# Other banks for layer one's first products, and another order of the steps, in a fused sigmoid attention and two-layer network

## The chip, the cores and the metric

The kernel runs on one core of one Trainium2 chip. The metric is device time in microseconds for one execution; the figure for the kernel before is the median of three runs.

## The reference

Shapes: `q`, `k`, `v` are 8 x 12 x 448 x 64 (batch, heads, sequence, head width), `w_in` is 768 x 2048, `w_out` 2048 x 768, `beta` 2048, all float32. The result is 3584 x 768, float32.

```python
scores = q @ k.transpose(0, 1, 3, 2) / sqrt(64) - log(448)
attn = 1.0 / (1.0 + exp(-scores))              # a sigmoid, no softmax
x = (attn @ v).transpose(0, 2, 1, 3).reshape(8 * 448, 12 * 64)
h = x @ w_in
g = h * (1.0 / (1.0 + exp(-beta * h)))         # swish with a beta for each column
out = g @ w_out
```

## The kernel before

Everything runs in float16 on TensorE (PE) with float32 sums in PSUM. Attention works on groups of four heads, three groups to a batch and 24 in all; group `g` lies in batch `g // 3`. Layer one and layer two run over batches and over tiles of 128 tokens. For the first tokens both layers are plain matrix products; from then on each layer uses a seven-product scheme for 2 x 2 blocks (P1 to P7, lines 377 to 595), which trades products for additions on VectorE (DVE).

The program is written as one list of steps, each of which emits some instructions. Each engine executes its own instructions in the order in which they were emitted, so the list sets the order of every queue at once: PE, DVE, ScalarE (ACT), GpSimd (POOL, which also issues the loads) and SyncE (SP, which issues the stores). A step's name is a letter and numbers:

- `V g.jt`: scores of group `g` for one block of keys into two score tiles, then two sigmoids on ACT (128 x 896 each). `A g`: the product of the weights with `v`, copied from PSUM by DVE.
- `D b.dc`: a plain layer-one product (`dense1`). `O t.half.part`: a plain layer-two product.
- `I b.d.i`: product P`i` of layer one for batch `b` and the pair `d` of column blocks (`wino1`): six matmuls of 224 columns, then an addition on DVE, a copy on ACT (P1) or two sigmoids (P2). `G b.d` and `B b.d.j` are the swish that follows, on ACT and POOL (`weigh_right`, `weigh_below`).
- `U t.i.part`: half of product P`i` of layer two for the tiles `t` and `t+1` (`wino2`): four matmuls of 384 columns, and after the second half an evacuation. P3 stores tile `t`, P4 stores tile `t+1`; so `U10.4.1` issues the stores of tile 11. A tile's store is four DMAs of 96 KB each, and one of 384 KB in the last batch. The last pair's P2 has one pass for each half of its columns (192 at a time).
- `H`, `X`, `S`, `T`: sums of operands for the seven-product scheme, on DVE. `R`: a transpose of `q` or `k` on DVE. `E`: a copy within `v`.
- `Q g`: the two loads of 224 KB for `q` and `k` of group `g`. `K b`: the six loads of `v` for batch `b` (144 and 48 KB). Both go out on POOL's queue.

PSUM has eight banks. During the opening three score tiles of two banks each are held, and two single banks. Then `share_psum(ctx, seconds, 2, N_ONE, 2)` divides them anew: two score tiles, and four single banks under the tags `one0` to `one3`. The function `bank` hands out the tag that has been unused for longest; with `first` = 2 the order begins with `one2`, `one3`, `one0`, `one1`. A tag gets its place in PSUM when its first tile is made, so here the tags got banks 0, 1, 2 and 3 in the order in which they were first asked for: `one2` got bank 0, `one3` bank 1, `one0` bank 2, `one1` bank 3. After the last V, `scores_done` gives the score tiles' four banks to the same pool, as `one4` to `one7`. A bank is held from a product's opening to the `release` in its last evacuation.

Output buffers (`osb`, four of them, pool `outp`) hold both layer one's partial results and layer two's output tiles; one comes free when its stores have landed. Groups of loaded `q` and `k` share three buffers, batches of `v` two.

In the opening, the eight loads of `w_in` (384 KB each) stand on POOL's queue behind the loads of the first batch. The first layer-one products (16 `dense1` of 224 columns, called by `first_half`) start with four, then three, with half visits of scores in between. A dense product's weights are put in one full 128-column load, or, when the next V or A after the step is an A, as two 64-column halves (`tiled`), the way A's own products are tiled.

Of the kernel before, what the change touches and what calls it, by code (L numbers as in the profile page):

```python
# [13 lines left out]
def kernel(  # L14
# [632 lines left out]
    STEPS = """
        R3.1 R3.0 D0.6 D0.12 R4.1 D0.14 D0.7 V3.1 R4.0 D0.13 D0.0 D0.8 V3.0 D0.3 D0.9 V3.3 D0.1
        D0.10 E1 D0.2 Q6 V3.2 D0.4 O0.0.0 D0.5 O0.0.1 O0.0.2 V4.1 O1.0.0 O0.0.3 A3 V4.0 O1.0.1 R5.1
        D0.11 D0.15 O0.0.4 R5.0 V4.2 O0.0.5 S1.1 O0.0.6 O1.0.2 O1.0.3 S1.0 O0.0.7 S2.0 O1.0.4 V4.3  # L650
        O1.0.5 A4 V5.1 O1.0.6 O0.1.0 O0.1.1 O1.1.0 S2.1 Q7 T3.1 O1.0.7 S4.0 T2.1 O0.1.2 V5.0 T3.0
        O0.1.3 O1.1.1 K2 O1.1.2 O1.1.3 O0.1.4 O0.1.5 V5.2 T2.0 O1.1.4 O0.1.6 O0.1.7 R6.1 O1.1.5 R6.0
        A5 O1.1.6 I1.3.1 V6.2 O1.1.7 S4.1 D1.8 R7.0 S3.1 D1.11 T1.1 Q8 V6.0 Q9 D1.3 R7.1 D1.2 X1.0
        V6.1 D1.10 D1.9 E2 K3 D1.1 X1.1 V6.3 T1.0 D1.0 A6 V7.1 I1.3.6 I1.3.2 X1.2 I1.3.5 V7.0 X1.3
        I1.3.7 I1.3.3 I1.2.1 I1.3.4 G1.3 I1.2.6 B1.3.0 V7.2 R8.1 I1.2.5 I1.2.7 R8.0 B1.3.1 I1.2.2
        I1.2.3 I1.2.4 V8.0 U2.1.0 H2.2 B1.2.1 B1.2.0 R9.1 U2.1.1 R9.0 A7 V8.1 H2.0 H2.1 T4.1 T4.0
        U2.7.0 U2.2.0 U2.2.1 Q10 V8.2 U2.5.0 U2.6.0 U2.6.1 X2.0 S3.0 H2.3 E3 V8.3 U2.5.1 A8 G1.2
        X2.1 V9.1 U2.7.1 U2.3.0 U2.3.1 H4.0 I2.0.1 R10.0 V9.2 H4.2 I2.0.6 U2.4.0 I2.0.5 U2.4.1
        I2.0.2 H4.1 I2.0.3 R10.1 X2.2 U4.1.0 V9.0 X2.3 U4.1.1 Q11 G2.0 U4.6.0 U4.6.1 Q12 A9 V10.0
        I2.0.7 H4.3 U4.5.0 U4.7.0 U4.5.1 V10.1 U4.7.1 I2.0.4 B2.0.1 U4.3.0 U4.4.0 U4.2.0 B2.0.0  # L660
        U4.2.1 R11.0 U4.3.1 U4.4.1 R11.1 I2.1.1 V10.2 Q13 Q14 I2.1.6 I2.1.5 I2.1.7 I2.1.2 K4 I2.1.3
        V10.3 I2.1.4 G2.1 B2.1.0 R12.1 I2.2.1 B2.1.1 A10 V11.0 I2.2.6 I2.2.5 R12.0 I2.2.7 I2.2.2
        I2.2.3 I2.3.1 Q15 G2.2 V11.1 I2.3.6 I2.2.4 B2.2.1 B2.2.0 I2.3.5 I2.3.2 R13.1 I2.3.7 I2.3.3
        V11.2 I2.3.4 B2.3.1 U6.1.0 B2.3.0 H6.2 U6.1.1 A11 H6.0 V12.2 U6.2.0 U6.7.0 H6.1 U6.2.1 G2.3
        V12.0 X3.0 U6.5.0 U6.6.0 U6.6.1 X3.1 U6.5.1 H6.3 I3.0.1 U6.7.1 I3.0.6 X3.2 V12.1 H8.0 E4
        R13.0 U6.3.0 U6.3.1 U6.4.0 U6.4.1 I3.0.5 R15.0 Q16 V12.3 H8.2 I3.0.2 A12 H8.1 V13.1 I3.0.3
        R14.0 U8.1.0 U8.1.1 U8.5.0 U8.6.0 G3.0 I3.0.7 U8.6.1 V13.0 X3.3 R15.1 H8.3 U8.2.0 R14.1
        U8.2.1 U8.5.1 U8.7.0 V13.2 U8.7.1 U8.3.0 I3.0.4 U8.4.0 R16.1 B3.0.0 B3.0.1 U8.3.1 V14.0
        U8.4.1 I3.1.1 A13 V14.1 I3.1.6 K5 I3.1.5 I3.1.7 I3.1.2 I3.1.3 I3.2.1 I3.1.4 Q18 I3.2.6 G3.1
        B3.1.0 B3.1.1 I3.2.2 I3.2.5 V14.2 I3.2.7 I3.2.3 Q17 I3.3.1 I3.2.4 G3.2 I3.3.6 I3.3.5 B3.2.0  # L670
        B3.2.1 I3.3.2 I3.3.7 I3.3.3 V14.3 I3.3.4 U10.1.0 B3.3.0 B3.3.1 H10.2 R16.0 U10.1.1 A14 V15.2
# [5 lines left out]
        U12.4.1 Q20 G4.1 V16.3 I4.1.4 A16 B4.1.0 B4.1.1 R19.0 V17.2 I4.2.1 I4.3.1 I4.2.6 I4.2.5
        V17.1 I4.2.2 Q21 I4.2.7 I4.2.3 G4.2 V17.0 I4.2.4 I4.3.6 B4.2.0 I4.3.5 I4.3.7 I4.3.2 B4.2.1
        R20.0 I4.3.3 G4.3 V18.2 I4.3.4 R19.1 A17 I5.0.1 B4.3.0 X5.0 B4.3.1 U14.1.0 V18.0 I5.0.2 X5.1
        I5.0.6 Q22 I5.0.5 U14.1.1 V18.1 X5.2 X5.3 H14.0 I5.0.3 U14.2.0 E6 H14.2 K7 I5.0.7 H14.1  # L680
        V18.3 G5.0 U14.2.1 A18 V19.2 I5.0.4 U14.6.0 U14.5.0 U14.7.0 B5.0.0 U14.6.1 U14.5.1 B5.0.1
        U14.7.1 I5.1.1 V19.0 H14.3 I5.1.6 I5.1.2 U14.3.0 R21.1 U14.3.1 R20.1 V19.1 U14.4.0 E7 I5.1.5
        I5.1.7 U14.4.1 I5.1.3 V20.0 R21.0 I5.1.4 G5.1 B5.1.0 I5.2.1 B5.1.1 A19 V20.2 I5.2.6 Q23
        I5.2.5 I5.2.2 I5.2.7 I5.2.3 I5.3.1 I5.2.4 G5.2 I5.3.6 B5.2.0 V20.3 I5.3.5 I5.3.7 B5.2.1
        I5.3.2 I5.3.3 I5.3.4 V20.1 X6.0 B5.3.1 H16.2 B5.3.0 U16.1.0 U16.1.1 A20 V21.2 U16.2.0 H16.0
        U16.7.0 U16.2.1 G5.3 V21.0 H16.1 U16.5.0 R23.1 U16.6.0 U16.6.1 H16.3 U16.5.1 U16.7.1 H18.2
        I6.0.1 X6.2 V21.1 U16.3.0 X6.1 U16.3.1 U16.4.0 U16.4.1 I6.0.6 R22.1 I6.0.2 R22.0 I6.0.5 A21
        V22.0 H18.0 X6.3 I6.0.3 H18.1 U18.1.0 U18.7.0 U18.1.1 V22.1 I6.0.7 U18.6.0 U18.6.1 V22.2
# [6 lines left out]
        X7.3 H22.2 H22.1 U20.4.1 U22.5.0 I7.0.6 I7.0.5 U22.7.0 I7.0.7 I7.0.3 U22.6.0 G7.0 I7.0.4
        I7.1.1 I7.1.6 I7.1.5 B7.0.0 B7.0.1 I7.1.2 I7.1.7 I7.2.1 I7.1.3 I7.2.6 G7.1 I7.1.4 I7.2.5
        I7.2.7 B7.1.0 B7.1.1 U22.6.1 I7.2.2 I7.2.3 U22.5.1 H22.3 I7.2.4 I7.3.1 I7.3.6 B7.2.0 I7.3.5
        G7.2 B7.2.1 I7.3.7 U22.7.1 I7.3.2 I7.3.3 U24.1.0 I7.3.4 U22.3.0 U22.3.1 U24.1.1 U22.4.0
        B7.3.0 U22.4.1 U24.2.0 B7.3.1 H24.0 U26.1.0 U24.2.1 H24.1 U24.5.0 G7.3 U24.6.0 H24.2 U24.6.1
# [138 lines left out]
```

## Time and profile before

| | |
|---|---|
| median of three runs | 369.06 us (368.25 to 369.5) |
| profiled execution | 368.85 us |
| its span | 367.1 us |
| PE busy | 360.9 us (98%), 3677 matmuls |
| DVE, ACT, POOL busy | 74%, 68%, 42% |
| granted PE clock | 0.999 |
| store of 96 KB, median issue to landing | 2.4 us (all stores: 1.8 to 6.8) |

The span runs from the first to the last instruction of the profiled execution; 1.75 us of its time lie outside. Start times in the profile's rows count from the start of the span. In a row of the timeline the bracket gives the idle time ahead of it and what ended that. In a row of windows there come the window, its length, and then busy time and instructions of PE, weight loads, DVE, ACT and POOL, the granted clock, the DMA share and GB/s. A row of the chain of waits gives start, duration, and the engine with its line. `L168` is the matmul of every dense product, so rows are told apart by their operands and times.

### The profile page before, as it was taken

What the parts mean: (1) busy time and instruction counts of PE and PEld (TensorE: products, weight loads), DVE (VectorE), ACT (ScalarE), POOL (GpSimd) and SP (SyncE); (2) the same over time, 40 slices, a digit from 0 to 9 for tenths busy, and PEclk for the clock granted to TensorE, in tenths of its full rate; (3) what the DMA queues carried; (4) which work ended last, traced back from release to release, by engine and by line L of the source; (5) the groups of instructions that cost most, each with busy time, mean ns of one, the idle gap of its engine ahead of it and who ended that gap; (6) DMA issues with size and microseconds to landing.
All of it is one profiled execution on the core that took longest, in us unless ns stands there. A gap on an engine that the chain in (4) does not pass through costs nothing.

```text
span 367.1 us, 9125 instructions
## 1 busy us (share of the span) xinstructions
PE 360.9 (98%) x3677; PEld 237.7 (65%) x3677; DVE 272.1 (74%) x521; ACT 249.0 (68%) x409; POOL 154.3 (42%) x192
## 2 busy tenths in 40 slices
...
GB/s 165 175 196 201 195 206 200 234 52 2 50 139 52 158 154 2 68 69 103 163 13 150 52 138 51 50 80 88 52 1 88 2 88 2 0 88 0 60 66 135
...
## 3 DMA queue, kind: packets, MB, share of 16 engines
...
q8 instruction: 29, 0.48, 0.5%
q14 instruction: 13, 0.11, 0.1%
...
## 4 chain that ended last, share of the span: by engine, by line
PE 89%; DMA 6%; POOL 1%; DVE 1%; ACT 1%; issue 0%; SPq 0%; ACTq 0%; DVEq 0%; POOLq 0%
PE m_ps L168 70%; PE sco L215 10%; PE av_ps L288 9%; DMA w_in<-in_moe_w_in_dram 3%; DMA raw<-in_k_dram 2%; DMA out_dram<-osb 1%; POOL w_in L150 1%; POOL raw L112 1%; DVE osb L369 0%; ACT attnT L227 0%; SPq L599 0%; ACT osb L422 0%; DVE xT L297 0%; DVE osb L564 0%; ACT osb L460 0%
## 5 line engine op out<-in xcount | busy, mean ns | idle before, releaser
L227 ACT ACTIVATE attnT<-sco 128x896 f16<-128x896 f32 (+1 forms) x163 | 139.2, 907 | 38.0 <-PE sco L215 37.3
L369 DVE TENSOR_TENSOR osb<-m_ps,osb 128x448 f32<-128x448 f32 (+2 forms) x197 | 116.4, 597 | 50.3 <-PE m_ps L168 41.5
L168 PEld LDWEIGHTS <-w_in 128*128 128x128 f16 (+1 forms) x948 | 80.7, 100 | 19.4 <-issue 11.0
L168 PE MATMUL m_ps<-xT,w_in 128*128 128x224 f16 (+3 forms) x750 | 85.7, 266 | 0.6 <-DVE xT L297 0.5
L489 POOL TENSOR_TENSOR gt<-osb,sg 128x448 f16<-128x448 f32 x26 | 29.6, 1137 | 117.7 <-ACT sg L422 107.8
L499 POOL TENSOR_TENSOR gt<-osb,sg 128x448 f16<-128x448 f32 x52 | 58.3, 1138 | 35.3 <-ACT sg L422 33.7
L422 ACT ACTIVATE sg<-osb,beta_sb 128x224 f32<-128x224 f32 (+1 forms) x104 | 54.0, 575 | 10.3 <-DVE osb L369 10.0
L168 PEld LDWEIGHTS <-sum 128*128 128x128 f16 (+1 forms) x444 | 39.9, 99 | 27.4 <-issue 3.6
L168 PEld LDWEIGHTS <-gt 128*128 128x128 f16 (+1 forms) x474 | 37.0, 102 | 25.8 <-issue 7.5
L168 PE MATMUL m_ps<-w_out,gt 128*128 128x384 f16 (+2 forms) x350 | 52.6, 324 | 0.1
L215 PE MATMUL sco<-qT,kT 32*128 32x448 f16 (+3 forms) x864 | 51.4, 340 | 0.7 <-DVE kT L201 0.6
L168 PEld LDWEIGHTS <-w_S 128*128 128x128 f16 (+1 forms) x486 | 43.9, 99 | 7.0 <-issue 6.0
L168 PE MATMUL m_ps<-w_out,sum 128*128 128x384 f16 (+1 forms) x228 | 40.6, 327 | 0.0
L168 PE MATMUL m_ps<-w_T,sum 128*128 128x384 f16 (+1 forms) x216 | 40.3, 327 | 0.0
L297 DVE CAST xT<-av_ps 128x448 f16<-128x448 f32 (+1 forms) x54 | 28.4, 567 | 14.1 <-PE av_ps L288 13.9
L288 PE MATMUL av_ps<-attnT,v 128*64 128x448 f16 (+3 forms) x400 | 38.2, 343 | 0.0
L168 PE MATMUL m_ps<-xs,w_S 128*128 128x224 f16 (+1 forms) x330 | 36.2, 260 | 0.0
L288 PEld LDWEIGHTS <-v 128*64 128x64 f16 (+1 forms) x432 | 20.4, 108 | 17.7 <-issue 9.8
L422 ACT ACTIVATE osb<-m_ps,beta_sb 128x224 f32<-128x224 f32 x52 | 20.5, 449 | 15.1 <-PE m_ps L168 14.0
L215 PEld LDWEIGHTS <-kT 32*128 32x128 f16 (+1 forms) x864 | 13.5, 96 | 23.2 <-issue 21.1
L460 ACT COPY osb<-m_ps 128x448 f32<-128x448 f32 x26 | 13.8, 536 | 17.7 <-PE m_ps L168 15.3
L317 DVE TENSOR_TENSOR gt<-m_ps,sg 128x224 f16<-128x224 f32 (+1 forms) x40 | 16.6, 434 | 12.1 <-ACT sg L314 11.9
...
## 6 DMA issues: line engine op xcount, KB each, us to landing
...
w_in<-in_moe_w_in_dram POOLq DMA_DIRECT2D x8, 384.0 KB, 11.1
w_out<-in_moe_w_out_dram POOLq DMA_DIRECT2D x4, 768.0 KB, 12.6
...
```

The source lines that it names most:

```text
L112: nc.gpsimd.dma_start(out=raws[g][:, r, c0:c1].rearrange("p c d -> p (c d)"), in_=(q, k)[r][b, HQ * t : HQ * (t + 1)].rearrange("h (p c) d ...
L168: nc.tensor.matmul(to[c : c + step], hidden[:, c : c + step], weights, **({} if step == P else {"tile_position": (0, c)}), **flags,)
L215: nc.tensor.matmul(sco[base : base + nk, hh, u0 : u0 + n], kT[g][lo : lo + BLK, jt * P : jt * P + nk, e], qT[g][lo : lo + BLK, c0 : c0 + n ...
L227: nc.scalar.activation(out=at[:, :, 0:n], in_=sco[:, :, 0:n], func=AF.Sigmoid, bias=NEG_LOG_S, scale=MSCALE,)
L288: nc.tensor.matmul(av[hh * D : (hh + 1) * D, 0:n], vs[b][base : base + nk, 2 * (s % NPAIR) + hh, jt], at[base : base + nk, hh, 0:n], start ...
L297: nc.vector.tensor_copy(out=xTs[b][:, s % NPAIR, c0 : c0 + n], in_=av[:, 0:n])
L317: nc.vector.tensor_tensor(out=gt[:, dc, off : off + n], in0=m1[:, 0:n], in1=sg[:, 0:n], op=ALU.mult)
L369: nc.vector.tensor_tensor(out=out, in0=in0, in1=in1, op=op)
L422: nc.scalar.activation(out=out, in_=in_, func=AF.Sigmoid, bias=0.0, scale=beta_sb[:, dc : dc + 1])
L460: nc.scalar.copy(out=oa[:, 0], in_=m)
L489: nc.gpsimd.tensor_tensor(out=gt[:, 2 * d : 2 * d + 2, off : off + QH], in0=ob[:, 0], in1=sg, op=ALU.mult)
L499: nc.gpsimd.tensor_tensor(out=gt[:, dc, off : off + S].rearrange("p (h n) -> p h n", h=2), in0=oa[:, :, j], in1=sg, op=ALU.mult,)
```

## The change

`share_psum` gets a loop that, where `first` is not zero (only the second call), makes one tile of each of the tags `one0` to `one3` in order, before any is used. So the tags lie in banks 0, 1, 2, 3 by their numbers, and the first products, which still ask for `one2` and `one3` first, lie in banks 2 and 3. In the opening the third score tile held these two; banks 0 and 1 were the two single ones.

The table `STEPS` holds the same 762 steps in another order. The parts that are spoken of below are shown; the rest is permuted in the same manner.

```diff
@@ share_psum
         used.clear()
         used.update(((i + first) % n_one, i - n_one) for i in range(n_one))
+        if first:
+            for i in range(n_one):
+                psum["one"].tile([P, S], FP32, tag=f"one{i}", name="place")
@@ STEPS
...
-        O1.0.5 A4 V5.1 O1.0.6 O0.1.0 O0.1.1 O1.1.0 S2.1 Q7 T3.1 O1.0.7 S4.0 T2.1 O0.1.2 V5.0 T3.0
...
-        V6.1 D1.10 D1.9 E2 K3 D1.1 X1.1 V6.3 T1.0 D1.0 A6 V7.1 I1.3.6 I1.3.2 X1.2 I1.3.5 V7.0 X1.3
...
-        I1.2.3 I1.2.4 V8.0 U2.1.0 H2.2 B1.2.1 B1.2.0 R9.1 U2.1.1 R9.0 A7 V8.1 H2.0 H2.1 T4.1 T4.0
...
-        R13.0 U6.3.0 U6.3.1 U6.4.0 U6.4.1 I3.0.5 R15.0 Q16 V12.3 H8.2 I3.0.2 A12 H8.1 V13.1 I3.0.3
-        R14.0 U8.1.0 U8.1.1 U8.5.0 U8.6.0 G3.0 I3.0.7 U8.6.1 V13.0 X3.3 R15.1 H8.3 U8.2.0 R14.1
-        U8.2.1 U8.5.1 U8.7.0 V13.2 U8.7.1 U8.3.0 I3.0.4 U8.4.0 R16.1 B3.0.0 B3.0.1 U8.3.1 V14.0
-        U8.4.1 I3.1.1 A13 V14.1 I3.1.6 K5 I3.1.5 I3.1.7 I3.1.2 I3.1.3 I3.2.1 I3.1.4 Q18 I3.2.6 G3.1
...
-        U10.2.0 H10.0 U10.7.0 H10.1 G3.3 U10.2.1 U10.5.0 U10.6.0 U10.6.1 H10.3 U10.5.1 X4.0 V15.0
-        U10.7.1 X4.1 U10.3.0 U10.3.1 I4.0.1 I4.0.6 I4.0.5 H12.0 U10.4.0 X4.2 U10.4.1 X4.3 I4.0.2
-        I4.0.3 I4.0.7 V15.1 E5 K6 G4.0 Q19 H12.2 U12.1.0 H12.1 U12.1.1 A15 R17.0 V16.1 U12.2.0 R18.1
...
-        I6.1.4 B6.1.0 I6.2.6 I6.2.5 B6.1.1 I6.2.2 V23.1 I6.2.7 I6.2.3 I6.3.1 I6.2.4 I6.3.6 G6.2
-        B6.2.1 I6.3.5 B6.2.0 I6.3.7 I6.3.2 I6.3.3 V23.2 I6.3.4 B6.3.1 U20.1.0 H20.2 U20.1.1 A23
-        U20.7.0 B6.3.0 U22.1.0 H20.0 U20.2.0 H20.1 X7.0 U20.2.1 U20.5.0 U20.6.0 G6.3 U20.6.1 I7.0.1
...
-        U24.5.1 H24.3 H26.0 U24.7.0 U24.7.1 U26.1.1 U24.3.0 U24.3.1 H26.1 U24.4.0 U26.2.1 U26.5.0
-        U26.6.0 H26.2 U26.6.1 U26.5.1 H26.3 U26.7.0 U26.7.1 U24.4.1 U26.3.0 U26.3.1 U26.4.0 U26.4.1
-        U26.2.0
...
+        V4.3 O1.0.5 A4 K2 V5.2 S2.1 O0.1.0 O1.1.0 O1.1.1 S4.1 O0.1.1 O0.1.2 O1.0.6 V5.0 O0.1.3
+        O0.1.4 O1.1.2 X1.0 T3.0 O1.0.7 O0.1.5 V5.1 O1.1.3 O1.1.4 T3.1 O0.1.6 T2.1 O0.1.7 A5 I1.2.1
...
+        I1.3.1 A6 V7.0 I1.2.7 I1.3.2 I1.3.6 R8.1 V7.1 I1.3.5 I1.2.4 I1.3.7 B1.2.0 I1.3.3 B1.2.1 V7.2
+        I1.3.4 U2.1.0 R8.0 U2.1.1 R9.1 R9.0 B1.3.0 B1.3.1 V8.0 A7 U2.2.0 V8.2 H2.2 U2.2.1 U2.7.0
...
+        E4 U6.4.0 H6.3 I3.0.2 R13.0 I3.0.5 U6.3.0 U6.3.1 I3.0.3 U6.4.1 V12.3 H8.0 H8.1 I3.0.7 A12
+        V13.1 I3.0.4 G3.0 Q16 U8.1.0 H8.2 U8.1.1 U8.6.0 U8.6.1 U8.5.0 R15.1 R14.1 U8.5.1 U8.7.0
+        V13.0 U8.2.0 H8.3 U8.2.1 U8.7.1 V13.2 U8.3.0 R14.0 B3.0.1 U8.3.1 U8.4.0 U8.4.1 B3.0.0 I3.1.1
+        R15.0 Q17 A13 V14.1 I3.1.6 I3.1.5 I3.1.2 I3.1.7 I3.1.3 K5 I3.2.1 I3.1.4 G3.1 B3.1.1 I3.2.6
...
+        A14 H10.1 V15.0 X4.0 R16.0 U10.2.0 Q19 R16.1 U10.2.1 G3.3 U10.5.0 Q18 I4.0.1 U10.6.0 U10.6.1
+        V15.1 X4.1 U10.5.1 I4.0.6 U10.7.1 I4.0.2 H10.3 E5 I4.0.5 H12.2 V15.2 U10.3.0 X4.2 I4.0.3
+        H12.0 X4.3 U10.4.0 U10.3.1 H12.1 U10.4.1 V16.0 I4.0.7 A15 V16.1 I4.0.4 K6 B4.0.1 U12.1.0
+        R17.1 U12.6.0 R18.1 U12.1.1 U12.6.1 U12.7.0 V16.2 U12.2.0 H12.3 R17.0 G4.0 B4.0.0 U12.5.0
...
+        G6.1 I6.1.4 I6.2.6 B6.1.0 I6.2.5 I6.2.7 B6.1.1 I6.2.2 V23.1 I6.3.1 I6.2.3 I6.2.4 B6.2.0 G6.2
+        I6.3.6 B6.2.1 I6.3.5 I6.3.7 I6.3.2 V23.0 I6.3.3 U20.1.0 I6.3.4 H20.2 U22.1.0 U20.1.1 B6.3.1
+        B6.3.0 A23 U20.7.0 U20.2.0 U20.2.1 H20.0 H20.1 X7.0 G6.3 I7.0.1 U20.5.0 U20.6.0 U20.6.1
...
+        U26.6.0 U26.6.1 U26.5.0 H26.3 U26.5.1 U24.4.0 U26.7.0 U26.3.0 U26.7.1 U26.3.1 U24.4.1
+        U26.4.0 U26.4.1 U26.2.0
```

More of the change, by code (lines that the diff above doesn't have):

```diff
@@ L647 @@
     STEPS = """
-        R3.1 R3.0 D0.6 D0.12 R4.1 D0.14 D0.7 V3.1 R4.0 D0.13 D0.0 D0.8 V3.0 D0.3 D0.9 V3.3 D0.1
-        D0.10 E1 D0.2 Q6 V3.2 D0.4 O0.0.0 D0.5 O0.0.1 O0.0.2 V4.1 O1.0.0 O0.0.3 A3 V4.0 O1.0.1 R5.1
-        D0.11 D0.15 O0.0.4 R5.0 V4.2 O0.0.5 S1.1 O0.0.6 O1.0.2 O1.0.3 S1.0 O0.0.7 S2.0 O1.0.4 V4.3
-        O1.0.5 A4 V5.1 O1.0.6 O0.1.0 O0.1.1 O1.1.0 S2.1 Q7 T3.1 O1.0.7 S4.0 T2.1 O0.1.2 V5.0 T3.0
-        O0.1.3 O1.1.1 K2 O1.1.2 O1.1.3 O0.1.4 O0.1.5 V5.2 T2.0 O1.1.4 O0.1.6 O0.1.7 R6.1 O1.1.5 R6.0
@@ L653 @@
-        A5 O1.1.6 I1.3.1 V6.2 O1.1.7 S4.1 D1.8 R7.0 S3.1 D1.11 T1.1 Q8 V6.0 Q9 D1.3 R7.1 D1.2 X1.0
-        V6.1 D1.10 D1.9 E2 K3 D1.1 X1.1 V6.3 T1.0 D1.0 A6 V7.1 I1.3.6 I1.3.2 X1.2 I1.3.5 V7.0 X1.3
-        I1.3.7 I1.3.3 I1.2.1 I1.3.4 G1.3 I1.2.6 B1.3.0 V7.2 R8.1 I1.2.5 I1.2.7 R8.0 B1.3.1 I1.2.2
-        I1.2.3 I1.2.4 V8.0 U2.1.0 H2.2 B1.2.1 B1.2.0 R9.1 U2.1.1 R9.0 A7 V8.1 H2.0 H2.1 T4.1 T4.0
-        U2.7.0 U2.2.0 U2.2.1 Q10 V8.2 U2.5.0 U2.6.0 U2.6.1 X2.0 S3.0 H2.3 E3 V8.3 U2.5.1 A8 G1.2
-        X2.1 V9.1 U2.7.1 U2.3.0 U2.3.1 H4.0 I2.0.1 R10.0 V9.2 H4.2 I2.0.6 U2.4.0 I2.0.5 U2.4.1
@@ L659 @@
[L659 to L664, printed above, removed]
@@ L665 @@
-        V12.0 X3.0 U6.5.0 U6.6.0 U6.6.1 X3.1 U6.5.1 H6.3 I3.0.1 U6.7.1 I3.0.6 X3.2 V12.1 H8.0 E4
-        R13.0 U6.3.0 U6.3.1 U6.4.0 U6.4.1 I3.0.5 R15.0 Q16 V12.3 H8.2 I3.0.2 A12 H8.1 V13.1 I3.0.3
-        R14.0 U8.1.0 U8.1.1 U8.5.0 U8.6.0 G3.0 I3.0.7 U8.6.1 V13.0 X3.3 R15.1 H8.3 U8.2.0 R14.1
-        U8.2.1 U8.5.1 U8.7.0 V13.2 U8.7.1 U8.3.0 I3.0.4 U8.4.0 R16.1 B3.0.0 B3.0.1 U8.3.1 V14.0
-        U8.4.1 I3.1.1 A13 V14.1 I3.1.6 K5 I3.1.5 I3.1.7 I3.1.2 I3.1.3 I3.2.1 I3.1.4 Q18 I3.2.6 G3.1
-        B3.1.0 B3.1.1 I3.2.2 I3.2.5 V14.2 I3.2.7 I3.2.3 Q17 I3.3.1 I3.2.4 G3.2 I3.3.6 I3.3.5 B3.2.0
@@ L671 @@
-        B3.2.1 I3.3.2 I3.3.7 I3.3.3 V14.3 I3.3.4 U10.1.0 B3.3.0 B3.3.1 H10.2 R16.0 U10.1.1 A14 V15.2
-        U10.2.0 H10.0 U10.7.0 H10.1 G3.3 U10.2.1 U10.5.0 U10.6.0 U10.6.1 H10.3 U10.5.1 X4.0 V15.0
-        U10.7.1 X4.1 U10.3.0 U10.3.1 I4.0.1 I4.0.6 I4.0.5 H12.0 U10.4.0 X4.2 U10.4.1 X4.3 I4.0.2
-        I4.0.3 I4.0.7 V15.1 E5 K6 G4.0 Q19 H12.2 U12.1.0 H12.1 U12.1.1 A15 R17.0 V16.1 U12.2.0 R18.1
-        I4.0.4 B4.0.0 U12.6.0 B4.0.1 U12.2.1 U12.5.0 V16.2 U12.6.1 U12.5.1 I4.1.1 H12.3 I4.1.6
-        U12.7.0 U12.7.1 R17.1 I4.1.5 U12.3.0 U12.3.1 I4.1.2 V16.0 R18.0 I4.1.3 U12.4.0 I4.1.7
@@ L677 @@
[L677 to L688, printed above, removed]
@@ L689 @@
-        I6.0.4 H18.3 U18.5.0 G6.0 U18.2.0 R23.0 U18.5.1 U18.2.1 B6.0.1 B6.0.0 U18.7.1 V22.3 U18.3.0
-        U18.3.1 U18.4.0 U18.4.1 I6.1.1 I6.1.6 A22 V23.0 I6.1.5 I6.1.7 I6.1.2 I6.1.3 I6.2.1 G6.1
-        I6.1.4 B6.1.0 I6.2.6 I6.2.5 B6.1.1 I6.2.2 V23.1 I6.2.7 I6.2.3 I6.3.1 I6.2.4 I6.3.6 G6.2
-        B6.2.1 I6.3.5 B6.2.0 I6.3.7 I6.3.2 I6.3.3 V23.2 I6.3.4 B6.3.1 U20.1.0 H20.2 U20.1.1 A23
-        U20.7.0 B6.3.0 U22.1.0 H20.0 U20.2.0 H20.1 X7.0 U20.2.1 U20.5.0 U20.6.0 G6.3 U20.6.1 I7.0.1
-        U20.5.1 H20.3 X7.2 U22.1.1 U20.7.1 I7.0.2 X7.1 U20.3.0 U20.3.1 U22.2.0 U22.2.1 H22.0 U20.4.0
@@ L695 @@
[L695 to L699, printed above, removed]
-        U24.5.1 H24.3 H26.0 U24.7.0 U24.7.1 U26.1.1 U24.3.0 U24.3.1 H26.1 U24.4.0 U26.2.1 U26.5.0
@@ L701 @@
-        U26.6.0 H26.2 U26.6.1 U26.5.1 H26.3 U26.7.0 U26.7.1 U24.4.1 U26.3.0 U26.3.1 U26.4.0 U26.4.1
-        U26.2.0
+        R3.1 R3.0 D0.7 D0.11 D0.0 R4.0 D0.3 V3.0 D0.4 D0.6 D0.14 R4.1 D0.9 V3.2 D0.2 D0.1 V3.3 D0.8
+        Q6 E1 D0.5 D0.12 V3.1 S1.0 D0.10 S2.0 O1.0.0 O1.0.1 O0.0.0 O1.0.2 V4.1 S1.1 Q7 O0.0.1 A3
+        R5.1 V4.2 O0.0.2 O1.0.3 D0.13 D0.15 V4.0 O0.0.3 R5.0 O0.0.4 O0.0.5 O0.0.6 S3.1 O1.0.4 O0.0.7
+        V4.3 O1.0.5 A4 K2 V5.2 S2.1 O0.1.0 O1.1.0 O1.1.1 S4.1 O0.1.1 O0.1.2 O1.0.6 V5.0 O0.1.3
@@ new lines @@
+        O0.1.4 O1.1.2 X1.0 T3.0 O1.0.7 O0.1.5 V5.1 O1.1.3 O1.1.4 T3.1 O0.1.6 T2.1 O0.1.7 A5 I1.2.1
+        R6.1 R6.0 X1.1 T1.0 O1.1.5 O1.1.6 O1.1.7 D1.3 D1.9 T2.0 Q8 I1.2.2 V6.0 I1.2.6 D1.8 I1.2.5 Q9
+        V6.1 T1.1 D1.11 D1.1 V6.2 R7.1 E2 R7.0 I1.2.3 D1.2 Q10 K3 D1.10 V6.3 X1.3 D1.0 G1.2 X1.2
+        I1.3.1 A6 V7.0 I1.2.7 I1.3.2 I1.3.6 R8.1 V7.1 I1.3.5 I1.2.4 I1.3.7 B1.2.0 I1.3.3 B1.2.1 V7.2
+        I1.3.4 U2.1.0 R8.0 U2.1.1 R9.1 R9.0 B1.3.0 B1.3.1 V8.0 A7 U2.2.0 V8.2 H2.2 U2.2.1 U2.7.0
@@ new lines @@
+        H2.0 H2.1 U2.5.0 V8.1 U2.6.0 T4.0 Q12 S4.0 X2.0 U2.6.1 U2.5.1 V8.3 H2.3 T4.1 U2.7.1 G1.3
+        R10.1 A8 V9.2 U2.3.0 U2.3.1 X2.1 X2.2 I2.0.1 S3.0 U2.4.0 V9.0 R10.0 I2.0.6 X2.3 I2.0.5
+        U2.4.1 E3 I2.0.2 I2.0.7 I2.0.3 H4.0 V9.1 U4.1.0 H4.2 I2.0.4 H4.1 A9 V10.2 U4.7.0 U4.1.1
+        U4.6.0 U4.6.1 U4.5.0 U4.5.1 U4.7.1 Q11 B2.0.1 G2.0 H4.3 V10.0 U4.2.0 U4.2.1 B2.0.0 U4.4.0
+        U4.3.0 U4.3.1 R11.0 I2.1.1 R11.1 V10.1 U4.4.1 I2.1.6 I2.1.5 K4 R12.0 I2.1.2 I2.1.7 I2.1.3
+        V10.3 I2.1.4 R12.1 B2.1.1 G2.1 Q13 I2.2.1 A10 V11.0 I2.2.6 B2.1.0 I2.2.5 I2.2.7 I2.2.2
```

27 lines of the change are left out of this document (added).

## The prediction

> **What bounds the kernel now.** I read the page's busy shares first, then the chain of waits, then what PE itself waited for, then the timeline where the table changes.
>
> ```profile
> PE 360.9 (98%) x3677; PEld 237.7 (65%) x3677; DVE 272.1 (74%) x521; ACT 249.0 (68%) x409; POOL 154.3 (42%) x192
> PE 89%; DMA 6%; POOL 1%; DVE 1%; ACT 1%; issue 0%; SPq 0%; ACTq 0%; DVEq 0%; POOLq 0%
> 24.60:363.60 339.00, 338.81 (x3414) 225.87 (x3406) 261.70 (x490) 230.73 (x383) 138.23 (x164) 1.00 0.52 88
> ```
>
> The third line is a window from just behind the opening to the last product: PE is busy 338.81 of 339.00 us at a granted clock of 1.00. An order of issue can take nothing from such a stretch except PE's stalls, and can only add new ones. So I look for stalls, and for what the opening waits for.
>
> ```profile
> 13.23 10.52 DMA w_in<-in_moe_w_in_dram
> 23.80 0.75 PE m_ps L168 x6
> ...
> 154.74 4.52 PE m_ps L168 x32
> 159.28 0.57 DVE osb L564
> 159.89 2.76 PE m_ps L168 x16
> ...
> 171.50 5.43 DMA out_dram<-osb
> 177.11 0.78 ACT osb L422 x2
> ...
> 181.37 0.73 PE m_ps L168 x6
> ```
>
> The chain leaves PE in three places that matter. At 23.80 the seventh product of layer one starts when a chunk of `w_in` lands. At 159.89 and 181.37 PE waits for an evacuation (DVE's copy of U8.1.1, then I3.3.3's adds) that had itself waited for an output buffer whose stores were still under way: Q16's loads stood beside the stores of U6.4.1 (5.8 to 6.5 us to landing, against 1.8 to 1.9 for those of U10.4.1, which had no load beside them), K5 and Q18 beside those of U8.4.1. Measured as excess over the usual spacing of matmul starts they are 0.21 us each; other spots (V3.3 0.06, some 0.04 four times) bring the sum of stalls behind the opening to 0.64 us.
>
> **Part one, the banks.** The loop adds no instruction; it fixes which memory the tags name. Before, tags got memory in order of first use.
>
> ```profile
> 18.99 0.39 DVE L297 CAST xT<-av_ps 128x224 f16<-128x224 f32 x1 [0.23 <-PE av_ps L288]
> 19.30 0.84 DVE L781 STREAM_TRANSPOSE beta_sb<-beta_in 32x32 f32<-32x32 f32 x4
> 19.43 1.41 PE L168 MATMUL m_ps<-xT,w_in 128*128 128x224 f16 x13 [0.48 <-DVE xT L297]
> 20.23 0.45 ACT L314 ACTIVATE sg<-m_ps,beta_sb 128x224 f32<-128x224 f32 x1 [1.13 <-PE m_ps L168]
> ```
>
> So the first product lay where the last `av_ps` was, and started 0.05 after the cast of 18.99 to 19.38 had read it (as an input that cast is read only by the sixth matmul of the product, 5 x 0.096 = 0.48 us in). After, it lies in a bank of the third score tile, whose sigmoids are done at 16.84 + 2.26 = 19.10, so it can start near 19.15: 0.28 earlier. I value that at nothing, because two waits stand behind it. The first sigmoid (20.23) needs `beta_sb`, done at 20.14, whatever PE does; and the seventh product can't start before 23.80, where the chunk lands (the load engines were busy since the start and POOL's order is unchanged there). PE waited 0.31 there; it will wait 0.59. Without that cover the gain would be the 0.28. The chunks behind it land at 26.3, 28.3, 30.3 and 32.3, close behind PE, so nothing is made up later.
>
> **Part two, the table.** The same 762 steps, permuted; DVE, ACT, POOL and SP run the same instructions as before. PE: steps between a V and the next A run as 64-column pairs, and the new order has 22 more matmuls for that. A pair costs what one full matmul does (96 ns for 224 columns, 163 for 384), but each entry from a dense product to scores costs about 0.1 us more and each exit as much. Summing the start-to-start intervals of every adjacent pair, taken class by class from the old trace, gives the new order +0.1 us.
>
> *Old stalls removed:* Q16 now stands behind G3.0 on POOL's queue, laid out some 4 us after U6.4.1's stores have gone, and the steps around the others differ: up to -0.64.
>
> *New stalls.* I laid the new order end to end, each instruction by its kind's mean duration and spacing in this trace. The two largest are late. In batch 6 the old table has I6.2.3, I6.3.1, I6.2.4, I6.3.6; the new has I6.2.3, I6.2.4, I6.3.6, with I6.3.1 ahead of all.
>
> ```profile
> 303.59 0.74 PE L168 MATMUL m_ps<-xT,w_S 128*128 128x224 f16 x6
> 303.79 1.27 DVE L369 TENSOR_TENSOR osb<-m_ps,osb 128x448 f32<-128x448 f32 x2 [0.93 <-PE m_ps L168]
> 304.17 0.74 PE L168 MATMUL m_ps<-xT,w_in 128*128 128x224 f16 x6
> 304.74 0.74 PE L168 MATMUL m_ps<-xs,w_in 128*128 128x224 f16 x6
> 305.32 0.93 PE L168 MATMUL m_ps<-xs,w_S 128*128 128x224 f16 x8
> ```
>
> These are those four products at 0.576 us each (6 x 96 ns). I6.3.6 opens the bank that I6.2.3 leaves, and it is free when DVE's add (0.62) has read it: last matmul's start 0.48, to DVE 0.30, 0.62, back 0.05: 1.45 us after I6.2.3 starts. Three products gave 1.73; two give 1.15. Stall: 0.30.
>
> The other is U22.1.0, now five steps after V23.0. With the visits over, it takes the first bank that the score tiles held, and V23.0's second tile is still to be read there: ACT has V23.0's two sigmoids (0.92 each) behind B6.2.0's, which wait for I6.2.4's add. By the layout ACT is through 6.7 us after I6.2.3's start, PE is there at 6.2 (the 0.30 included): 0.56 with the hand-over. Before, U20.1.1, A23 and U20.7.0 stood ahead of it. Smaller: V5.1, with only two steps to V5.0 where each visit needs two score tiles read (0.13), V7.1 and V8.0 0.03 each. Sum 1.05.
>
> *The end.* U24.4.1 stores a whole tile.
>
> ```profile
> L599 SPq DMA_DIRECT2D out_dram<-osb x105: 314/421/1568, 63.9 to 364.1; - x105
> DMA to landing us min/median/max: 1.8/2.5/6.8
> ```
>
> The 1568 ns is that issue; it began at 360.3 with U26.3 and U26.4 still to run. Now only U26.4.0, U26.4.1 and U26.2.0 come behind U24.4.1, some 2.0 us (4 + 4 matmuls at 0.163, 8 at 0.082), and SP comes to the last stores late: +0.22. The last landing beside 384 KB could cost up to 1.0 (the page has 3.6 us to landing for 384 KB, 2.6 for 192 KB); I take 0, since the large one leaves first.
>
> *Loads beside stores.* Elsewhere the new places of Q and K are between 0 and the rival below; I take +0.15, near the lower end, since most stores get free stretches.
>
> Weighed against one rule: the Trainium skill, Perfetto Trace Analysis, Identifying the Most-Contended Engine, says that matmul busy time is a poor measure and that weight-load busy time is the better one. By its 65% a new order could gain much; the rows above (a product every 0.576 us, no gap) show TensorE streaming, so I give it no term.
>
> **Sum:** +0.1 - 0.64 + 1.05 + 0.22 + 0.15 = +0.9 us. The profiled execution took 368.85 (span 367.1 and 1.75 around it), 0.21 under the median of 369.06; so 369.75 by the profile, 370.0 for the median. Measurement can tell about 0.3%, 1.1 us.
>
> **Rivals.**
>
> *B, slower: stores of U10.4.1 caught by K6.* U12.1.1's copy reuses the buffer that U10.4.1 stores. Four stores of 96 KB go out near 201 us; laid out, PE waits one for one once they take more than 3.0 us to land. Alone they took 1.9. Before, K6 went out at 190.2 with nothing ahead; now Q18's 448 KB are issued just ahead of it on POOL's queue (which runs ahead of PE here, so K6 leaves before U10.4.1 although the list has it behind) and K6 leaves some 2 us later: its last issue is near 195, and with 4.8 us to landing as before, or the 6.0 that the page has for such pieces, it is down at 200 to 201. At the 3.3 to 3.9 us of U10.3.1's stores before, which had K6 beside them, +0.3 to +0.9; at U6.4.1's 5.8 to 6.5, +2.8 to +3.5. I take the near row's end, +0.9: 370.9. It decides once K6's last piece lands after 201. Against it: the old stores with K6 just gone took 1.9.
>
> A rule beside it: the Trainium skill, DMA: Bandwidth & Descriptors, Queues, rings and completion order, has each DMA engine take turns between the queues that it has work for; equal turns would double 1.9 us to an estimated 3.8, +0.8. U10.3.1's rows agree; U6.4.1's tripled time doesn't, so the larger end stays in the range.
>
> *C: the two late stalls don't come.* If the score tiles lie the other way round in the late banks, or ACT has a little more room than I gave it, U22.1.0 is free at once; with an add's usual overlap I6.3.6 also loses its 0.30. -0.86: 369.1.
>
> *D: the change does what its first part says on the path.* If the first product's 0.28 passes through (the `w_in` chunks landing earlier) and both late stalls are also absent: 368.8. The DMA row of 10.52 us speaks against it.
>
> **Chances.** Forecast 0.45, B 0.28, C 0.15, D 0.06, a visit that waits longer for its score tiles than laid out 0.06. An error of some 0.5 us in the sum of stalls puts 0.10 of the forecast over +1.1; of B 0.26 lies there, and the last case whole: slower 0.42. Faster needs D or C with that error on top: 0.08. Same 0.50. The range reaches down to D less 0.6 for the error of the sum, 368.2, and up to 372.0, between B's two prices; its far end I leave out, since it needs K6 beside the stores on their whole way.
>
> **What would show it.** In the new profile: PE busy 98% again; the first `m_ps` near 19.15 and the seventh product still near 23.8; no wait of U8.2.0 on L564; a PE gap of about 0.3 at I6.3.6 and 0.5 at U22.1.0, the second with ACT's sigmoid L227 as releaser; the last 1.57-us issue of SP beginning about 362.4. If the opening's first sigmoid or the seventh product moves forward, part one is wrong; if `out_dram<-osb` shows as releaser of U12.1.1's copy, B holds; if PE has a gap over 0.6 that I haven't named, the layout failed there.

## The result

| | before | after |
|---|---|---|
| median of 20 runs | 368.73 us (368.19 to 369.5) | 369.76 us (369.09 to 371.39) |
| ratio to before | | 1.0029, 95% interval 1.0019 to 1.0039 |
| profiled execution, span | 368.85, 367.1 us | 370.58, 368.8 us |

The kernel after is slower by 1.03 us (0.29% by the ratio); the forecast sum was +0.88, written as 370.0 against 369.06. So the size came out, but part of it for the wrong reasons, as the experiments show. Profile against profile it did not: 370.58 us, where the forecast had 369.75 for the profiled execution.

The page of the kernel after, busy shares and chain, and the same kind of window as before, from behind the opening to the last product:

```profile
PE 362.4 (98%) x3699; PEld 237.9 (65%) x3699; DVE 272.2 (74%) x521; ACT 248.4 (67%) x409; POOL 154.0 (42%) x192
PE 87%; DMA 6%; ACT 2%; POOL 2%; DVE 1%; issue 1%; SPq 0%; ACTq 0%; DVEq 0%; POOLq 0%
24.60:365.20 340.60, 339.21 (x3431) 225.79 (x3428) 261.18 (x490) 230.12 (x383) 137.88 (x164) 1.00 0.53 88
```

PE was idle for 0.19 us of this stretch before and is for 1.39 now; ACT and POOL hold 2% of the chain each, where they held 1%. The stretch itself is longer by more, since PE that waits for a bank can show as busy with the matmul ahead of it; so a gap below is what a step's matmul starts come late, by the usual spacing for each pair of shapes in the trace of before, added up over the step. (Some expectations below name 0.39 us for V5.1 and 0.75 for V20.3; these added up single matmuls of a step of which later ones catch up. By the step they are 0.21 and 0.61. U22.1.0's 0.62 is that of its first matmul; the step comes to 0.65.)

The chain of waits between 170 and 182 us:

```profile
170.50 0.45 SPq L602
...
171.00 6.19 DMA out_dram<-osb
...
177.38 0.52 ACT osb L425 x2
...
181.64 0.73 PE m_ps L171 x6
```

This stands in the place of the row of 171.50 before: U8.4.1's last store takes 6.19 us (5.43 before), I3.2.2's sigmoids wait for its buffer, and PE loses 0.23 us at I3.3.2 and 0.81 at I3.3.3, where it lost 0.21 before. The forecast had it gone.

The timeline at the end of batch 6, PE and then ACT:

```profile
305.04 0.74 PE L171 MATMUL m_ps<-xT,w_S 128*128 128x224 f16 x6
305.61 0.74 PE L171 MATMUL m_ps<-xs,w_in 128*128 128x224 f16 x6
306.56 1.31 PE L171 MATMUL m_ps<-xs,w_S 128*128 128x224 f16 x12 [0.21 <-DVE osb L372]
...
311.91 1.49 PE L171 MATMUL m_ps<-w_out,gt 128*64 128x384 f16 x16 [0.46 <-ACT attnT L230]
```

```profile
310.14 1.71 ACT L230 ACTIVATE attnT<-sco 128x896 f16<-128x896 f32 x2
```

Here are the two stalls that were laid out: I6.3.6 starts 306.56 - 305.61 = 0.95 us after I6.2.4 instead of 0.576 (stall 0.37, forecast 0.30), and U22.1.0 at 311.91, 0.06 after ACT has read V23.0's second score tile at 311.85 (stall 0.65, forecast 0.56).

The opening, PE's timeline of the kernel after:

```profile
18.40 0.69 PE L291 MATMUL av_ps<-attnT,v 128*64 128x224 f16 x8
19.31 2.46 PE L171 MATMUL m_ps<-xT,w_in 128*128 128x224 f16 x24 [0.21 <-ACT attnT L230]
```

The first product waits 0.21 us for the score tile's sigmoid, where it waited 0.48 for a cast. In this execution the seventh product again waited for its chunk, by 0.26. (By the measure of the step, which takes in the delay of the first matmul beside the engine's idle time, the first product's two waits are 0.28 and 0.55 us.)

### The profile page after: what moved, and what is told of

Read it like the earlier page. It is cut to its first block, busy times and chain, and to the rows that moved or that the text cites. A ratio compares the mean times of both kernels' runs of the same rounds, so it can differ in the third digit from the quotient of the medians.

```text
span 368.8 us, 9179 instructions
## 1 busy us (share of the span) xinstructions
PE 362.4 (98%) x3699; PEld 237.9 (65%) x3699; DVE 272.2 (74%) x521; ACT 248.4 (67%) x409; POOL 154.0 (42%) x192
## 4 chain that ended last, share of the span: by engine, by line
PE 87%; DMA 6%; ACT 2%; POOL 2%; DVE 1%; issue 1%; SPq 0%; ACTq 0%; DVEq 0%; POOLq 0%
PE m_ps L171 67%; PE sco L218 10%; PE av_ps L291 9%; DMA w_in<-in_moe_w_in_dram 3%; DMA raw<-in_k_dram 2%; DMA out_dram<-osb 2%; ACT sg L425 1%; ACT attnT L230 1%; DVE osb L372 1%; POOL w_in L153 1%; POOL raw L115 1%; POOL gt L502 1%; ACT osb L425 0%; SPq L602 0%; ACT osb L463 0%
## 5 line engine op out<-in xcount | busy, mean ns | idle before, releaser
L171 PE MATMUL m_ps<-xT,w_in 128*128 128x224 f16 (+3 forms) x768 | 84.8, 266 | 0.4 <-ACT attnT L230 0.2
L136 POOL DMA_DIRECT2D v<-in_v_dram x32 | 19.9, 636 | 13.4 <-DMA w_out<-in_moe_w_out_dram 6.8
```

What stands on the lines that cost most here:

```text
L136: nc.gpsimd.dma_start(out=vs[b][i * BLK : (i + 1) * BLK, :, 0:JF].rearrange("p h j d -> p h (j d)"), in_=rows[:, :, JF * i * D : JF * (i + ...
L171: nc.tensor.matmul(to[c : c + step], hidden[:, c : c + step], weights, **({} if step == P else {"tile_position": (0, c)}), **flags,)
```

## Experiments

Theory: PE is the bound, so the change is worth the sum of its stalls; the late ones come from hand-offs of banks, the one near 180 us from loads beside stores, and the opening's gain ends at the `w_in` chunk. Rivals: the banks themselves cost or win, stalls that are removed turn up elsewhere, or SP and not the loads makes the stores late. Every kernel was timed against the kernel before on its own chip, so ratios are what compares; kernels behind the first four were chosen after those.

| kernel | median us | ratio to before | interval | gaps in its profile, us |
|---|---|---|---|---|
| loop, old table | 368.45 | 0.9991 | 0.9981 to 1.0002 | U8.2.0 0.11 |
| same, again | 368.47 | 0.9986 | 0.9973 to 0.9998 | U8.2.0 0.35, I3.2.2 and I3.3 0.73 |
| new table, no loop | 369.78 | 1.0027 | 1.0015 to 1.0039 | V5.1 0.21, I3.3 0.73, I6.3.6 0.37, U22.1.0 0.65 |
| after, again | 369.59 | 1.0018 | 1.0006 to 1.0031 | V5.1 0.21, I3.3 0.36, I6.3.6 0.37, U22.1.0 0.65 |
| end of batch 6 repaired | 369.06 | 1.0005 | 0.9990 to 1.0019 | V5.1 0.21, I3.3 0.97 |
| K5 later | 370.08 | 1.0036 | 1.0023 to 1.0049 | V5.1, I6.3.6, U22.1.0 as after; U10.5 and U10.7 0.61 |
| K5 early | 369.37 | 1.0016 | 1.0007 to 1.0025 | V5.1, I6.3.6, U22.1.0 as after; I5.3 and V20.3 0.61 |
| K5 and K7 early | 369.45 | 1.0007 | 0.9997 to 1.0017 | V5.1, I6.3.6, U22.1.0 as after |
| repairs, K5 early | 368.34 | 0.9990 | 0.9982 to 0.9999 | I5.3 and V20.3 0.74 |
| old table freed | 368.33 | 0.9984 | 0.9974 to 0.9993 | O0.0.0 0.54 |
| repairs, K5 and K7 early | 368.05 | 0.9983 | 0.9973 to 0.9993 | none over 0.08 |

### The loop alone, twice

```diff
 (the table of before)
+        if first:
+            for i in range(n_one):
+                psum["one"].tile([P, S], FP32, tag=f"one{i}", name="place")
```

> The kernel before with the loop in share_psum alone, its table unchanged. Theory (the opening waits for a w_in chunk anyway): the first layer-one product starts about 0.28 us sooner after the last av_ps product than before, the seventh product still starts when its chunk lands (23.6 to 23.8), and the time is that of before within 0.15 us. Rival (the gain is carried through): 0.28 us less, and a seventh product 0.28 us earlier. Other rival (the banks change a hand-off later on): a new PE gap behind the opening, a time over 0.3 us longer.

Both medians lie under before, by 0.39 and 0.49 us; the first run's interval still reaches 1.0002. The profile of that run shows a reason; PE's timeline:

```profile
19.29 2.46 PE L171 MATMUL m_ps<-xT,w_in 128*128 128x224 f16 x24 [0.21 <-ACT attnT L230]
21.68 0.58 PE L218 MATMUL sco<-qT,kT 32*128 32x224 f16 x16
22.19 1.90 PE L171 MATMUL m_ps<-xT,w_in 128*128 128x224 f16 x18
24.02 0.65 PE L218 MATMUL sco<-qT,kT 32*128 32x224 f16 x12
```

Eighteen matmuls in 24.02 - 22.19 = 1.83 us: the seventh product (from 23.35) doesn't wait at all. From the first product to the seventh are 4.06 us, against 4.37 in the profile of before. The chunk landed at 22.70 us here and at 23.75 in the profile of before, where POOL had issued the first `w_in` load at 10.71 instead of 9.90; why POOL was later there isn't shown. Of the 13 profiles of this study only the first two, before and after, show a wait of the seventh product for its chunk. The other eleven come from three other sessions on three chips (14, 7 and 4), and the chip of the first two isn't on record, so it stays open whether the execution or the chip decides. So the theory of the opening fell, and the run was repeated with the other one written down:

> The table of before with the loop, once more on another chip. Theory now (the seventh product waited for its chunk in two of the profiles and not in the others, so the first product's 0.28 us reaches the end in most executions): 0.2 to 0.4 us under before, the interval of the ratio below 1.000, no wait of the seventh product in the profile. Rival (the first theory, the chunk always absorbs it): the time of before within 0.15 us.

The interval now lies under 1. Its profiled execution took 369.09 against a median of 368.47, with stalls of 1.08 us at U8.2.0, I3.2.2 and I3.3; the same table showed 0.11 in the first run. The stalls of stores beside loads are no constants of an order.

### The new table without the loop

```diff
 (the table of after)
-        if first:
-            for i in range(n_one):
-                psum["one"].tile([P, S], FP32, tag=f"one{i}", name="place")
```

> The kernel after without the loop, so the new table with the old banks. Theory: the whole change in time is the table's, so 1.0 us over before (0.7 to 1.4), the same as after, with the first product 0.5 us behind the last av_ps product again. The banks of one0 to one3 differ, yet the order of tags is the same, so the gaps at V5.1, I3.3.3, I6.3.6 and U22.1.0 stay. Rival (the loop's banks make the late gaps): the gaps of I6.3.6 and U22.1.0 are gone and the time is that of before.

It keeps the three hand-off gaps of after to 0.01 us and is 0.94 us over before. The first product comes 0.55 us late by the step, as in before. That it isn't slower than after by the loop's 0.28 lies within the intervals. The table makes the loss; the banks make none of it.

### The end of batch 6

```diff
-  V23.1 I6.3.1 I6.2.3 I6.2.4 B6.2.0 G6.2 I6.3.6 B6.2.1 I6.3.5 I6.3.7 I6.3.2 V23.0 I6.3.3 U20.1.0 I6.3.4 H20.2 U22.1.0 U20.1.1 B6.3.1 B6.3.0 A23 U20.7.0
+  V23.1 I6.2.3 I6.3.1 I6.2.4 B6.2.0 G6.2 I6.3.6 I6.3.5 I6.3.7 I6.3.2 V23.0 B6.2.1 I6.3.3 U20.1.0 I6.3.4 H20.2 U20.1.1 B6.3.1 B6.3.0 A23 U20.7.0 U22.1.0
```

> The kernel after with three moves at the end of batch 6: I6.2.3 ahead of I6.3.1 again, so that two products stand between it and I6.3.6; U22.1.0 behind U20.7.0; B6.2.1 behind V23.0. Theory: the gaps of 0.37 us at I6.3.6 and 0.62 us at U22.1.0 go and nothing takes their place: 0.8 to 1.0 us under after, so 368.8 to 369.0, level with before within 0.2 us. Rival (the bank is late for whoever comes next): A23 or U20.1.1 waits 0.3 to 0.6 us instead and less than half is won. Rival (PE's lead is given back at the end): PE's gaps go, but the time stays at that of after.

Both gaps are gone and only 0.08 us at U20.6.0 is new. The median, 369.06, is just over the forecast range. It lies 0.70 us under after's median of 20 (by the ratios 0.24% or 0.9 us) and 0.53 under that of after's second measurement (by the ratios 0.13% or 0.5 us), against 1.02 us of gaps; in its own profile I3.3 still had 0.97. The first rival (A23 or U20.1.1 waits instead) is out. Against the other (the end gives it back) the comparison within one chip is stronger: the two kernels with K5 and K7 early, further down, differ by this repair, V5.1's and Q17's place, and by 1.40 us.

### K5 behind the stores

```diff
-  I3.1.3 K5 I3.2.1 I3.1.4 G3.1 B3.1.1 I3.2.6 B3.1.0 I3.2.5
+  I3.1.3 I3.2.1 I3.1.4 G3.1 B3.1.1 I3.2.6 B3.1.0 K5 I3.2.5
```

> The kernel after with one move: K5's six loads go behind B3.1.0, some 7 us later on POOL's queue, so that only Q17's loads stand beside U8.4.1's stores. Theory (the loads slow these stores, whose buffer I3.2.2's sigmoids need): the stores land in 2 to 4 us where the profile of after has up to 6.2, the PE gaps at I3.3.2 and I3.3.3 fall from 1.05 us to under 0.2, and the time is 0.4 to 0.9 us under after. Rival (SP issues them late, one issue of 1.69 us in front): the stores' landing time falls but the gap stays over 0.5 us, and the time is that of after. Rival (K5 itself comes too late then): a new gap near A15 or E5.

Half a miss. U8.4.1's last store landed at 174.66 instead of 177.19 (it was issued at 170.30, so SP wasn't the cause), I3.2.2's sigmoids started at 175.37 with no wait, and the gap at I3.3 was gone. But the time was no better, and the profile shows a price that no theory had: POOL issues the loads itself. POOL's timeline, and then DVE's:

```profile
177.47 2.50 POOL L136 DMA_DIRECT2D v<-in_v_dram  x4
179.96 1.22 POOL L143 DMA_DIRECT2D v<-in_v_dram  x2
181.18 1.16 POOL L492 TENSOR_TENSOR gt<-osb,sg 128x448 f16<-128x448 f32 x1
182.28 4.88 POOL L502 TENSOR_TENSOR gt<-osb,sg 128x448 f16<-128x448 f32 x4
```

```profile
182.66 1.32 DVE L372 TENSOR_TENSOR sum<-gt 128x1024 f16<-128x1024 f16 x1
...
187.19 0.69 DVE L372 TENSOR_TENSOR sum<-gt 128x1024 f16<-128x1024 f16 x1 [2.75 <-POOL gt L502]
187.80 1.15 DVE L300 CAST xT<-av_ps 128x448 f16<-128x448 f32 x2
```

K5's 3.7 us of issuing stand right ahead of five products of 1.1 us, DVE's H10 sum waits 2.75 us for the last, the casts of A14 queue behind that sum, and U10.5.0 waits for their bank (0.39 us). U10.7.0's 0.22 has another course: the sum H10.2, which it reads, took 1.32 us beside POOL's products, where it took 0.68 with K5 early and no product beside it. These 0.61 us don't explain the whole time: they are less than the 1.04 us at I3.3 in the profile of after, and the profiled execution was the fastest of the ten (369.68). Why the median is 370.08 isn't shown.

### K5 ahead of the stores

```diff
-  G3.0 Q16 U8.1.0 H8.2
+  G3.0 Q16 K5 U8.1.0 H8.2
```
(and K5 taken out behind I3.1.3)

> The kernel after with one move: K5's six loads go in front of the stores, directly behind Q16 (about 160 us, where POOL has nothing else to do for some 6 us), instead of beside U8.4.1's stores. Theory (loads slow those stores, and K5 moved later cost time only since its 3.7 us of issuing held up the products of G and B on POOL): no gap at I3.3.2 and I3.3.3, none at U10.5.0 or U10.7.0 either, 0.5 to 1.0 us under after. Rival (POOL's queue was not the cause of the new gaps, Q17's place beside the stores is): gaps at U10.5.0 or I3.3.3 of over 0.3 us remain. Rival (the next stores are caught instead): U8.3.1's stores land late and U8.2 to U8.5 show a gap; no gain.

The gap at I3.3 is gone without any at U10: K5 went out from 160.4 to 164.3, into POOL's idle time, and U8.4.1's last store landed at 174.76. The ratio fell from 1.0029 and 1.0018 (after, twice) to 1.0016; on the same chip the median is 0.22 us under after's, less than the theory's 0.5 and within the intervals. A new gap of 0.61 us stood at I5.3 and V20.3. It is the same mechanism in batch 5; these are rows of the chain in the kernel with all repairs, which has it too:

```profile
251.60 7.59 DMA out_dram<-osb
...
259.21 0.04 ACTq L425
...
259.28 0.04 ACTq L425
...
259.37 0.79 ACT osb L425 x2
```

U14.4.1's last store takes 7.59 us beside K7 and Q23, and I5.2.2 waits. In the kernel after it landed at 258.09 and wasn't waited for, as PE came to I5.2.2 only at 258.41. With K5 early it landed at 258.10, but PE was there at 256.92 (257.02 with all repairs). What was won at 180 us was in part given back at 260.

### The repairs together

```diff
 (the three moves at the end of batch 6, K5 behind Q16, and)
-  Q17 A13 V14.1
+  A13 V14.1
-  I3.2.6 B3.1.0 I3.2.5
+  I3.2.6 B3.1.0 Q17 I3.2.5
-  V5.1 O1.1.3 O1.1.4
+  O1.1.3 V5.1 O1.1.4
```

> The kernel after with K5 behind Q16, Q17 behind B3.1.0, V5.1 behind O1.1.3 and the three moves at the end of batch 6 (I6.2.3 ahead of I6.3.1, U22.1.0 behind U20.7.0, B6.2.1 behind V23.0). Theory (the stalls add up): gaps of 1.05, 0.39, 0.37 and 0.62 us gone, which is 2.4 us less than the profiled execution of after and, since the first varies from run to run, 1.6 to 2.2 us less than its median: 367.6 to 368.2, under before by 0.5 to 1.1. Rival (PE's time is only shifted to other waits): over 368.6, no better than before.

Just above the range and under the rival's bound: 368.34, with 0.74 us at I5.3 and V20.3 left. V5.1's gap went with one step between.

### The old table, freed

```diff
 (the table of before, with the loop)
-  R15.0 Q16 V12.3
+  R15.0 V12.3
-  U8.6.0 G3.0 I3.0.7
+  U8.6.0 G3.0 Q16 K5 I3.0.7
-  V14.1 I3.1.6 K5 I3.1.5
+  V14.1 I3.1.6 I3.1.5
-  I3.1.4 Q18 I3.2.6 G3.1 B3.1.0 B3.1.1 I3.2.2
+  I3.1.4 I3.2.6 G3.1 B3.1.0 B3.1.1 Q18 I3.2.2
```

> The table of before with the loop, Q16 moved behind G3.0, K5 behind Q16 and Q18 behind B3.1.1, so that no load stands beside the stores of U6.4.1 and U8.4.1. Theory: the gaps at U8.2.0 and I3.3.3 (0.21 us each in the profile of before) go; with the opening's gain 0.4 to 0.7 us under before, 368.1 to 368.4. Rival (the gaps are the order's own and not the loads'): they remain, and the time is that of the loop alone.

As forecast: both gaps gone, 368.33, and U8.4.1's stores landed in 1.8 to 1.9 us. A wait of 0.54 us at O0.0.0 shows in this profile and in no other; its cause wasn't followed.

### After, once more

> The kernel after unchanged, beside the others on one chip. Theory (the size of the gap at I3.3.2 and I3.3.3 and the landing of the w_in chunks vary from one execution to the next, the rest doesn't): gaps at V5.1, I6.3.6 and U22.1.0 within 0.03 us of the first profile, the other two different; median 369.6 to 369.9.

The three hand-off gaps repeat to 0.01 us; the gap at I3.3 was 0.36 instead of 1.04, with U8.4.1's last store landing at 176.45 instead of 177.19. The median, 369.59, lies at the lower end of the forecast.

### K7 and Q23 too

```diff
 (K5 behind Q16, and)
-  U14.6.0 Q22 V19.0
+  U14.6.0 Q22 K7 V19.0
-  I5.1.5 K7 I5.1.7 Q23 R22.0
+  I5.1.5 I5.1.7 R22.0
-  B5.1.1 B5.1.0 V20.1
+  B5.1.1 B5.1.0 Q23 V20.1
```

> The kernel after with the loads alone moved: K5 behind Q16 as in the run before, and now K7 behind Q22 (POOL is idle there from 238.4 to 244 us) and Q23 behind B5.1.0, so that nothing stands beside the stores of U14.3.1 and U14.4.1 either. Theory (the gap of 0.75 us at I5.3.5 and V20.3 in the profile with K5 early is the same mechanism further on: I5.2.2's sigmoids wait for U14.4.1's stores beside K7 and Q23): these stores land in 1.8 to 2.6 us, no gap at I5.3 or V20.3, and 0.3 to 0.7 us under the run with K5 early alone (369.37): 368.7 to 369.1. Rival (the gap comes from another wait, or from a single odd execution): the gap stays, or it goes and the median stays at 369.4.

The mechanism held: U14.4.1's stores took 1.8 to 1.9 us, and no gap of this kind is left. The number missed: 369.45, no better than with K5 early alone by the median, though on a chip where before took 368.96, so that the ratio fell from 1.0016 to 1.0007, which would be 0.33 us, with intervals that overlap. The single runs lie between 369.09 and 369.52 where after's lie between 369.09 and 371.39 (369.28 and 370.95 when it was measured again): across chips, this suggests that the loads cost mostly the upper half of the runs.

The last kernel has all the repairs and these three moves:

```diff
 (as in "The repairs together", and)
-  U14.6.0 Q22 V19.0
+  U14.6.0 Q22 K7 V19.0
-  I5.1.5 K7 I5.1.7 Q23 R22.0
+  I5.1.5 I5.1.7 R22.0
-  B5.1.1 B5.1.0 V20.1
+  B5.1.1 B5.1.0 Q23 V20.1
```

> All repairs of the run before (K5 behind Q16, Q17 behind B3.1.0, V5.1 behind O1.1.3, I6.2.3 ahead of I6.3.1, U22.1.0 behind U20.7.0, B6.2.1 behind V23.0), with K7 behind Q22 and Q23 behind B5.1.0. Theory: PE has no stall over 0.1 us behind the opening, 0.3 to 0.7 us under the 368.34 of the run without the last two moves: 367.6 to 368.0, the lowest of all. Rival (something else in the load order gives it back, R23 or E7 waiting for loads that are now late): a new gap behind 262 us, and 368.3 or more.

The best kernel of the study: 368.05 us, 0.9983 (0.9973 to 0.9993), just over the forecast range, 0.9 us under before on its chip, by ratio level with the old table freed. Against the kernel with only its loads moved, on the same chip, it wins 1.40 us; V5.1, I6.3.6 and U22.1.0 had 1.23 us of gaps there. Its window from behind the opening to the end:

```profile
24.60:363.00 338.40, 338.35 (x3418) 225.36 (x3414) 261.20 (x491) 229.89 (x382) 137.59 (x162) 1.00 0.53 88
```

PE is idle for 0.05 us in 338.4, and its weight loads are busy for 225.36 us, 67%: the share that the prediction weighed and gave no term left nothing here for an order to take.

## Why the prediction held, and where it didn't

**The bound.** PE's stalls did set the time: in the profiles nearly all of the difference is found in them. The last product starts 1.89 us later in the profile of after than in that of before, and the gaps and the 22 additional matmuls give 1.75 of it: +1.02 late, +0.33 at V5.1, V7.1 and V8.0, +1.04 at I3.3, -0.65 for the stalls of before, -0.09 in the opening, +0.1 for the pairs; the rest lies in pieces under 0.05. The medians differ by 1.03 only, mainly because I3.3's gap varies: the second profile of after had 0.68 us less there and took 369.84 us against 370.58.

**The late stalls**, forecast 0.86, measured 1.02, each within 0.09, with the releasers that were named. For I6.3.6 most of the excess is a wait that the layout didn't have: I6.2.3's add was laid out for 305.82 and began at 305.88, and the trace names POOL's product, which ended at 305.86, as what it waited for last. Taking both gaps out brought 0.5 to 0.9. Rival C is out.

**V5.1** was right in its place and too small: 0.13 forecast, 0.21 measured; V7.1 and V8.0 came at 0.05 and 0.07 for 0.03 each.

**The opening**, valued at nothing, was the step that failed. The cover was the `w_in` chunk at 23.75, read from one execution; in 11 of 13 profiles the chunk is there in time, and from the first product to the seventh are 4.06 us instead of 4.37. The `beta_sb` wait stayed as forecast, but it holds ACT and no product. So in most of these profiles nothing takes the gain of 0.28 us back, as rival D had it, and the loop alone brought 0.4 to 0.5 in two runs, one of them with an interval that just reaches 1.

**Loads beside stores** was the term that was sized wrong: +0.15, and for I3.3 a stall gone. In the four profiles of the new table with its own load order it is 0.36, 0.73, 0.97 and 1.04 us, while the old table has anything from 0.11 to 1.08 in the three profiles with its own order. Rival B had this mechanism at the wrong place. U12.1.1's copy ran at 205.34, not held up; K6's last piece landed at 202.80, past the point that was named, but U10.4.1's stores, issued from 202.22, still took 1.8 to 1.9.

**The tail**, +0.22, was nothing: from the last matmul's start to the end of the span are 3.70 us before and 3.53 after, and 3.52 to 3.55 in the other eleven profiles, with either table. The 1568 ns had been taken for the price of a 384 KB store. It was that store's issue (at 361.0 us; 360.3 is the start of the row with the stores ahead of it), but not its price: it took 0.92 to 1.57 us in the four profiles of the old table and 0.33 in all nine of the new. Among the stores of the profile after, 1.69 and 1.76 us are found at 167.4 and 154.2 us, on stores of 96 KB, and none of the last five takes over 0.36:

```profile
L602 SPq DMA_DIRECT2D out_dram<-osb x5: 332/347/356, 362.9 to 365.9; - x5
```

So two terms that were too high (the tail, and an opening valued at nothing: 0.5 us) met one that was too low (the loads) and hand-offs that were 0.3 us short in all, and the sum came out at +0.88 for +1.03. The late hand-offs were understood; that the rest cancelled to within 0.15 us is luck.

**The rule of turns.** The Trainium skill, DMA: Bandwidth & Descriptors, Queues, rings and completion order, has each DMA engine take turns between the queues that it has work for; equal turns would double a store's time of 1.9 us to an estimated 3.8. The last stores of U8.4.1 and U14.4.1 measured 5.4 to 7.6 beside two groups of loads, so the estimate from equal turns is too low there; beside Q17 alone U8.4.1's last took 4.4 to 4.8 in three profiles.
